# Softcapped attention with two feed-forward blocks: batches of three key chunks, the sums' transfers on GpSimd's queue, and a new order of VectorE's work at the end of attention

## The chip, the cores and the metric

The kernel runs on one core of a Trainium2 chip. The metric is the device time of one execution in microseconds (us), as the median of the runs. Times of single instructions come from one execution that the hardware profiler recorded; they count from the start of its span. The engines are called TensorE (PE in the profile; PEld is its loading of weights), VectorE (DVE), ScalarE (ACT), GpSimd (POOL) and SyncE (SP).

## What is computed

```
scores = (q @ k.T) / sqrt(64)                 # q, k, v: (2, 12, 448, 64), f32
scores = cap * tanh(scores / cap)             # cap = 30
attn   = exp(scores - max); attn /= attn.sum() + 1e-9
x      = attn @ v, laid out as 896 tokens x 768
x      = square(relu(x @ w_in)) @ w_out       # 768 -> 2048 -> 768
x      = silu(x @ w2_in) @ w2_out             # 768 -> 2048 -> 768
```

## The kernel before

Since the cap bounds the scores, the kernel leaves the maximum out: it takes exp(cap * tanh) and adds a constant, `gcap`, to the sums of the exponentials. The 24 heads are 12 pairs, i = 0 to 11. The 448 keys of a pair fall into three chunks of 128 and one of 64; the 64 last keys of two pairs share one chunk. So two pairs, one u = 0 to 5, have seven chunks, n = 0 to 6: n = 0 to 2 are the first pair's, n = 3 is the short shared one, n = 4 to 6 are the second pair's. There are 42 chunks, numbered here 0 to 41 (chunk 7u + n).

The order of the work is written out by hand. `batches` cuts the 42 chunks into 21 batches of two, and the loop over h goes one step per batch:

- `scores` (L274): TensorE multiplies keys and queries of a batch's chunks into tiles `s`, of which there are two (two PSUM banks each). ScalarE then runs tanh on each chunk (L282, from `s` to a tile `e` in SBUF), and after all chunks of the batch exp on each (L285, in place). A chunk's product must wait until the tanh of the chunk two before it has read its `s`.
- `evacuate` (L356): VectorE copies the finished product `px` of a pair that ended two steps ago to SBUF (`sb`).
- `add` (L315, L318, L321): VectorE adds the `e` of a pair together into `tot`, so that fewer products are needed for the sums.
- `values` (L296): TensorE multiplies the `e` of the batch before with the values into `px`.
- `add_up` (L333; L339 for the last two pairs) and `evacuate_sums` (L365): TensorE sums `tot` and the third `e` over the keys by a product with ones, VectorE copies the row of sums to `sm`, and SP's queue gathers it into a small tile `st` (L371), 56 numbers in each of 32 partitions for a group of two pairs.
- `invert` (L379 to L382) and `fetch` (L389), two steps after a group's second pair: VectorE forms the reciprocal of the small tile, SP's queue writes it to `scratch` in DRAM, and, once that has landed, reads it back spread over the partitions as `rb`.
- `normalise` (L396 to L399), some steps later: VectorE multiplies `sb` with `rb` and splits the result into two parts, `x0`, the input of the first feed-forward block.
- Up to two steps of the conversion of the first weights `u_wa` (L127 to L146), from 64-bit to 32-bit floats.

`GROUPS` holds the pairs 0 to 9. For pairs 10 and 11 (`LATE`) the sums are made in all partitions (L339) and inverted there, 128 x 448, on VectorE (L361, L362). On SP's queue the loads of the next queries, keys and values (L223, L224, L231) and of weights (L162) stand in one row with the sums' transfers; each instruction in it starts when the one ahead has been issued. After the loop follow the last products, sums and normalisations, and the first feed-forward block (L579) takes the first three units for the first batch entry alone (pairs 0 to 5).

Of the kernel before, what the change touches and what calls it, by code (L numbers as in the profile page):

```python
# [13 lines left out]
ALU = mybir.AluOpType  # L14
# [13 lines left out]
def softcap_attention_relu2_silu(  # L28
# [30 lines left out]
    NH = B * H  # L59
    GROUPS = ((0, 2), (2, 4), (4, 6), (6, 8), (8, 10))  # L60
    LATE = 10
    SCALE = 1.0 / float(D) ** 0.5
# [170 lines left out]
    def attention_bounded(att, ws, x0):  # L233
# [23 lines left out]
        parts = [(u, n) for u in range(NP2 // 2) for n in range(NU)]  # L257
        batches = [parts[n : n + 2] for n in range(0, len(parts), 2)]

# [7 lines left out]
        def scores(batch):  # L267

            for u, n in batch:
                sp = bank2(f"s{u}_{n}")  # L270
                for i, rows, keys in pieces(u, n):
                    for j in range(2):
                        p = slice(64 * j, 64 * j + 64)
                        nc.tensor.matmul(  # L274
                            sp[rows, j, :S],
                            lhsT=pr.qk[i][p, 1, keys],
                            rhs=pr.qk[i][p, 0],
                            start=True,
                            stop=True,
                        )  # L280
                t = att.tile([128, 2, S], F32, tag="e", bufs=7, name=f"e{u}_{n}")
                nc.scalar.activation(t, sp[:, :, :S], AF.Tanh, scale=scale_s)  # L282
                ex[u, n] = t
            for u, n in batch:
                nc.scalar.activation(ex[u, n], ex[u, n], AF.Exp, scale=scale_c)  # L285
# [18 lines left out]
        def add(batch):  # L304
            for u, n in batch:
                i = pieces(u, n)[0][0]
                e = ex[u, n]
                if i == NP2 - 1:
                    if n == NU - 1:
                        t = att.tile([128, 2, S], F32, tag="tot", bufs=3, name=f"tot{i}")  # L310
                        nc.vector.tensor_tensor(t, ex[u, n - 1], e, op=ALU.add)
                        tot[i] = [ex[u, NF + 1], t]
                elif n in (1, NF + 2):
                    t = att.tile([128, 2, S], F32, tag="tot", bufs=3, name=f"tot{i}")
# [10 lines left out]
        def add_up(i):  # L325
# [11 lines left out]
            for n, t in enumerate(tot[i]):  # L337
                for j in range(2):
# [6 lines left out]
                    )  # L345

        group = {i: gi for gi, (a, z) in enumerate(GROUPS) for i in range(a, z)}

# [9 lines left out]
        def evacuate_sums(i):  # L358
# [11 lines left out]
            for n in range(2):  # L370
                nc.sync.dma_start(  # L371
                    st[gi][8 * r : 8 * r + 16, n],
# [3 lines left out]
        def invert(gi):  # L376
# [4 lines left out]
            nc.vector.reciprocal(t, t)  # L381
            nc.sync.dma_start(scratch[2 * a : 2 * z].rearrange("r (a f) -> (r a) f", a=8), t)  # L382

        def fetch(gi):
# [3 lines left out]
            for j in range(2):  # L388
                nc.sync.dma_start(t[64 * j : 64 * j + 64], rows[j : j + 1].to_broadcast([64, z - a, S]))  # L389
            for i in range(a, z):  # L390
# [15 lines left out]
        todo = []  # L406
        loads = {0: 0, 2: 1, 4: 2, 8: 3, 12: 4, 16: 5}
        conversions = {4: 0, 8: 1, 12: 2}
        nb = len(batches)
# [6 lines left out]

        for h in range(nb + 1):
            if h < nb:
                scores(batches[h])
                for u, n in batches[h]:  # L420
                    if u + 1 < NP2 // 2:
                        if n in (1, 2):
                            pr.load(2 * u + 1 + n)
                        if n == 2:
                            pr.load_v(u + 1, FIRST)
                        if n == NF + 1:
                            pr.load_v(u + 1, SECOND)
                    if (u, n) == (0, 0):
                        pr.load_v(0, SECOND)
            if h == 1:  # L430
# [6 lines left out]
            for i in ended:  # L437
                evacuate(i)
            if h == nb:
                for i in ended:  # L440
                    add_up(i)
                add(batches[h - 1])
                due(h)
                break
            if h > 0:
                add(batches[h - 1])
                values(batches[h - 1])
                if (NP2 // 2 - 1, NF + 1) in batches[h - 1]:

                    e, u = ex[NP2 // 2 - 1, NF + 1], NP2 // 2 - 1  # L450
                    nc.vector.tensor_tensor(e[64:], e[64:], ex[u, NF][64:], op=ALU.add)
            for i in ended:
                add_up(i)
                evacuate_sums(i)
                for gi, (a, z) in enumerate(GROUPS):
                    if i == z - 1:
                        todo.append((lambda gi=gi: invert(gi), h + 2))
                        todo.append((lambda gi=gi: fetch(gi), h + 2))
                        for n in range(a, z):
                            todo.append((lambda n=n: normalise(n), h + 4 + 2 * (n - a)))  # L460
            if h in loads:
                ws.load_to(loads[h])
            due(h)
            if h in conversions:
                ws.convert_to(conversions[h], False)
                ws.split_to(conversions[h], False, nc.vector)
            if h == 16:
                ws.convert_to(3, False)
            ws.step(2)
        i = NP2 - 1  # L470
        values(batches[-1])
        add_up(i)
        evacuate_sums(i - 1)
        normalise(i - 1)
        due(99)
        evacuate_sums(i)
        sb[i] = px.pop(i)[:, :S]
# [251 lines left out]
```

## Time and profile before

| | us |
|---|---|
| median of 3 runs | 570.29 (568.53 to 572.13) |
| the profiled execution, its time | 571.89 |
| its span, first to last instruction | 570.1 |
| TensorE busy | 557.8 (98%) |
| VectorE busy | 409.6 (72%) |
| ScalarE busy | 251.3 (44%) |
| GpSimd busy | 1.0 (0%) |

Attention takes the span's first 97.56 us, then the feed-forward blocks begin. A view by windows gives for each stretch the busy time of each engine and the clock granted to TensorE (1.00 is 2.4 GHz, 0.50 is 1.2 GHz). The timeline lists instructions in order of time, neighbours of one kind merged into one line with their count; in brackets is how long the engine sat idle before, and what ended that. The chain of waits follows the work back from the last instruction to what released it.

### The profile page before, as it was taken

What the parts mean: (1) busy time and instruction counts of PE and PEld (TensorE: products, weight loads), DVE (VectorE), ACT (ScalarE), POOL (GpSimd) and SP (SyncE); (2) the same over time, 40 slices, a digit from 0 to 9 for tenths busy, and PEclk for the clock granted to TensorE, in tenths of its full rate; (3) what the DMA queues carried; (4) which work ended last, traced back from release to release, by engine and by line L of the source; (5) the groups of instructions that cost most, each with busy time, mean ns of one, the idle gap of its engine ahead of it and who ended that gap; (6) DMA issues with size and microseconds to landing.
All of it is one profiled execution on the core that took longest, in us unless ns stands there. A gap on an engine that the chain in (4) does not pass through costs nothing.

```text
span 570.1 us, 7396 instructions
## 1 busy us (share of the span) xinstructions
PE 557.8 (98%) x2896; PEld 469.8 (82%) x2896; DVE 409.6 (72%) x617; ACT 251.3 (44%) x376; POOL 1.0 (0%) x6
## 2 busy tenths in 40 slices
PE   9999897999999999999999999999999999999996
PEld 3323233999999999999999999999999999999996
DVE  1679999879988877667665768888888885547501
ACT  6998891156444443332332444454445522222101
POOL 0000000000000000000000000000000000000000
PEclk9999998999999999999999999999999999999999
DMA  8535550313333223333334443333343464345002
GB/s 271 170 96 159 170 170 19 85 56 112 110 112 111 75 74 112 103 119 116 105 94 148 124 154 91 102 102 103 109 109 108 110 166 119 105 155 164 1 0 102
DMA packets 51429, 64.30 MB, mean 113 GB/s; under 512 B 2746, under 2 KB 46522, under 8 KB 51386
## 3 DMA queue, kind: packets, MB, share of 16 engines
q1 hardware_dynamic: 51064, 63.36, 37.0%
q8 instruction: 24, 0.39, 0.3%
q10 hardware_dynamic: 290, 0.39, 0.2%
q14 instruction: 19, 0.16, 0.1%
q0 software_dynamic: 32, 0.00, 0.0%
HBM read 60.88 MB, written 2.79 MB: 112 GB/s over the span
## 4 chain that ended last, share of the span: by engine, by line
PE 89%; DVE 5%; DMA 4%; issue 1%; SPq 0%; ACT 0%; ACTq 0%; DVEq 0%
PE o_2f L658 6%; PE o_0f L658 6%; PE ha_0f L579 5%; PE ha_1f L579 5%; PE y_0f L579 5%; PE y_1f L579 5%; PE hc_1f L579 5%; PE hc_0f L579 5%; PE y0f L579 3%; PE y2f L579 3%; PE y4f L579 3%; PE o_6f L658 3%; PE o_5f L658 3%; PE o_4f L658 3%; PE s L274 2%; PE px L296 2%
## 5 line engine op out<-in xcount | busy, mean ns | idle before, releaser
L282 ACT ACTIVATE e<-s 128x896 f32<-128x896 f32 x42 | 36.8, 918 | 12.4 <-PE s L274 8.4
L285 ACT ACTIVATE e<-e 128x896 f32<-128x896 f32 x42 | 37.7, 955 | 0.0
L608 DVE TENSOR_TENSOR ra_0f<-ra_0f 128x448 f32<-128x448 f32 x16 | 9.9, 622 | 7.9 <-ACT ra_0f L606 7.9
L676 DVE COPY ob_0f<-o_0f 128x384 f32<-128x384 f32 x2 | 1.1, 558 | 17.2 <-PE o_0f L658 17.2
L606 ACT ACTIVATE rc_0f<-hc_0f 128x448 f32<-128x448 f32 x8 | 4.4, 546 | 20.1 <-PE hc_0f L579 20.1
L315 DVE TENSOR_TENSOR tot<-e,e 128x896 f32<-128x896 f32 x11 | 11.9, 1084 | 0.5 <-ACT e L285 0.5
L674 ACT ACTIVATE ob_1f<-o_0f 128x384 f32<-128x384 f32 x2 | 1.0, 492 | 25.6 <-PE o_0f L658 25.6
L606 ACT ACTIVATE ra_0f<-ha_0f 128x448 f32<-128x448 f32 x8 | 4.3, 542 | 16.8 <-PE ha_0f L579 16.8
L396 DVE TENSOR_TENSOR rb<-sb,rb 128x448 f32<-128x448 f32 x10 | 6.2, 622 | 6.2 <-DMA rb<-scratch 5.0
L141 ACT ACTIVATE hl_wb_2f<-u_wb_2f 128x512 fp32r<-128x512 f32 x6 | 3.8, 632 | 15.0 <-DVE u_wb_2f L134 15.0
L608 DVE TENSOR_TENSOR ra_1f<-ra_1f 128x448 f32<-128x448 f32 x16 | 9.9, 619 | 0.6 <-ACT ra_1f L606 0.6
L141 ACT ACTIVATE hl_wb_3f<-u_wb_3f 128x512 fp32r<-128x512 f32 x6 | 3.8, 632 | 14.8 <-DVE u_wb_3f L134 14.8
L333 PE MATMUL sum<-tot,ones 128*32 128x448 f32 x40 | 9.5, 551 | 0.0
L333 PE MATMUL sum<-e,ones 128*32 128x448 f32 x40 | 9.5, 551 | 0.0
L141 ACT ACTIVATE hl_wb_0f<-u_wb_0f 128x512 fp32r<-128x512 f32 x6 | 3.8, 630 | 12.5 <-DVE u_wb_0f L134 12.5
L639 ACT ACTIVATE x1f<-y_0f 128x448 fp32r<-128x448 f32 x3 | 1.6, 546 | 14.8 <-PE y_0f L579 14.8
L640 DVE TENSOR_TENSOR x1f<-y_0f,x1f 128x448 fp32r<-128x448 f32 x3 | 1.9, 624 | 8.4 <-ACT x1f L639 8.4
L579 PE MATMUL ha0f<-x0f,hl_wa0f 128*128 128x448 f32 x36 | 7.7, 368 | 0.0
L579 PEld LDWEIGHTS ha0f<-x0f,hl_wa0f 128*128 128x128 f32 x36 | 6.7, 188 | 1.2 <-issue 0.7
L579 PE MATMUL ha2f<-x0f,hl_wa2f 128*128 128x448 f32 x36 | 7.6, 365 | 0.0
L579 PE MATMUL hc4f<-x1f,hl_wc4f 128*128 128x448 f32 x36 | 7.5, 365 | 0.0
L579 PE MATMUL ha6f<-x0f,hl_wa6f 128*128 128x448 f32 x36 | 7.5, 365 | 0.0
(987 smaller groups left out, 1738.6 us busy)
## 6 DMA issues: line engine op xcount, KB each, us to landing
raw_wb_0f<-in_moe_w_out SPq DMA_DIRECT2D x6, 512.0 KB
raw_wb_1f<-in_moe_w_out SPq DMA_DIRECT2D x6, 512.0 KB
raw_wb_2f<-in_moe_w_out SPq DMA_DIRECT2D x6, 512.0 KB, 3.6
raw_wb_3f<-in_moe_w_out SPq DMA_DIRECT2D x6, 512.0 KB
rb<-scratch SPq DMA_DIRECT2D x10, 224.0 KB
raw_wd_0f<-in_moe_w_out SPq DMA_DIRECT2D x2, 768.0 KB
raw_wd_1f<-in_moe_w_out SPq DMA_DIRECT2D x2, 768.0 KB
raw_wd_2f<-in_moe_w_out SPq DMA_DIRECT2D x2, 768.0 KB
```

The source lines that it names most:

```text
L141: first = lambda: nc.scalar.activation(hl[:, 0], u, AF.Copy)
L274: nc.tensor.matmul(sp[rows, j, :S], lhsT=pr.qk[i][p, 1, keys], rhs=pr.qk[i][p, 0], start=True, stop=True,)
L282: nc.scalar.activation(t, sp[:, :, :S], AF.Tanh, scale=scale_s)
L285: nc.scalar.activation(ex[u, n], ex[u, n], AF.Exp, scale=scale_c)
L296: nc.tensor.matmul(px[i][64 * j : 64 * j + 64, :S], lhsT=pr.vt[u][rows, n, j], rhs=ex[u, n][rows, j], start=first, stop=last,)
L315: nc.vector.tensor_tensor(t, ex[u, n - 1], e, op=ALU.add)
L333: nc.tensor.matmul(sums[i][p : p + 32, :S], lhsT=ones[:, :32], rhs=t[:, j], start=True, stop=True)
L396: nc.vector.tensor_tensor(r, sb.pop(i), r, op=ALU.mult)
L579: nc.tensor.matmul(a, lhsT=hl[:, e_w, kk], rhs=mv[:, e_x], start=(first and e_w == 0 and e_x == 0), stop=(last and e_w == 1),)
L606: nc.scalar.activation(r, accs[f][b], func)
L608: nc.vector.tensor_tensor(r, r, r, op=ALU.mult)
L658: nc.tensor.matmul(acc[t], lhsT=g2[kf][:, e_g, t * 128 : t * 128 + 128], rhs=hl[:, e_w, kk], start=(kf == 0 and e_g == 0 and e_w == 0), st ...
```

## The change

A batch has three chunks, so the loop has 14 steps. There are ten tiles `e` and not seven; `s` keeps two. The sums' transfers of the first four groups (pairs 0 to 7) go to GpSimd's queue. `invert` and `fetch` come one step after a group's second pair, `normalise` three and four steps after, with the last ones held to steps 13 and the end. Loads and conversions of weights stand at other steps, three conversion steps to a step. Pair 10 is a group of its own with the small reciprocal. Pair 11's `tot` is formed as the others' are. Behind the loop the order is written anew.

```diff
-    GROUPS = ((0, 2), (2, 4), (4, 6), (6, 8), (8, 10))
-    LATE = 10
+    GROUPS = ((0, 2), (2, 4), (4, 6), (6, 8), (8, 10), (10, 11))
+    LATE = 11
...
-        batches = [parts[n : n + 2] for n in range(0, len(parts), 2)]
+        batches = [parts[n : n + 3] for n in range(0, len(parts), 3)]
...
-                t = att.tile([128, 2, S], F32, tag="e", bufs=7, name=f"e{u}_{n}")
+                t = att.tile([128, 2, S], F32, tag="e", bufs=10, name=f"e{u}_{n}")
...
-                if i == NP2 - 1:
-                    if n == NU - 1:
-                        t = att.tile([128, 2, S], F32, tag="tot", bufs=3, name=f"tot{i}")
-                        nc.vector.tensor_tensor(t, ex[u, n - 1], e, op=ALU.add)
-                        tot[i] = [ex[u, NF + 1], t]
-                elif n in (1, NF + 2):
+                if n in (1, NF + 2):
...
+        def queue(gi):
+
+            return nc.gpsimd if gi < 4 else nc.sync
...
-                nc.sync.dma_start(
+                queue(gi).dma_start(
                     st[gi][8 * r : 8 * r + 16, n],
...
-            nc.sync.dma_start(scratch[2 * a : 2 * z].rearrange("r (a f) -> (r a) f", a=8), t)
+            queue(gi).dma_start(scratch[2 * a : 2 * z].rearrange("r (a f) -> (r a) f", a=8), t)
...
-                nc.sync.dma_start(t[64 * j : 64 * j + 64], rows[j : j + 1].to_broadcast([64, z - a, S]))
+                queue(gi).dma_start(t[64 * j : 64 * j + 64, : z - a], rows[j : j + 1].to_broadcast([64, z - a, S]))
...
-        loads = {0: 0, 2: 1, 4: 2, 8: 3, 12: 4, 16: 5}
-        conversions = {4: 0, 8: 1, 12: 2}
+        loads = {0: 0, 1: 1, 3: 2, 6: 3, 8: 4}
+        conversions = {3: 0, 5: 1, 8: 2}
...
-            if h == nb:
-                for i in ended:
-                    add_up(i)
-                add(batches[h - 1])
-                due(h)
-                break
...
-                        todo.append((lambda gi=gi: invert(gi), h + 2))
-                        todo.append((lambda gi=gi: fetch(gi), h + 2))
+                        todo.append((lambda gi=gi: invert(gi), h + 1 if gi < 4 else nb))
+                        todo.append((lambda gi=gi: fetch(gi), h + 1 if gi < 4 else nb))
                         for n in range(a, z):
-                            todo.append((lambda n=n: normalise(n), h + 4 + 2 * (n - a)))
+                            at = h + 3 + n - a
+                            if at > nb - 2:
+
+                                at = nb - 1 if n == a and gi < 4 else nb
+                            todo.append((lambda n=n: normalise(n), at))
...
-            ws.step(2)
+            ws.step(3)
         i = NP2 - 1
+        last = GROUPS[-2]
+        add_up(i - 1)
+        add(batches[-1])
         values(batches[-1])
         add_up(i)
+
+        todo = [f for f, _ in todo]
+        late = [todo.pop() for _ in range(last[1] - last[0])][::-1]
+        inverted = [todo.pop() for _ in range(2)][::-1]
+        for f in inverted:
+            f()
+        evacuate(i - 1)
         evacuate_sums(i - 1)
+        for f in todo:
+            f()
+        invert(len(GROUPS) - 1)
+        fetch(len(GROUPS) - 1)
+        evacuate_sums(i)
+        for f in late:
+            f()
         normalise(i - 1)
-        due(99)
-        evacuate_sums(i)
         sb[i] = px.pop(i)[:, :S]
         normalise(i)
```

Three places show how the instructions stand. First TensorE at the end of the loop before: products of scores (`s`), with values (`px`) and with ones (`sum`), the last of u = 5, chunks 38 to 41.

```order
L274 MATMUL s_3_728<-qk10f 64x448 x2
L274 MATMUL s_3_728<-qk11f 64x448 x2
L274 MATMUL s_4_735<-qk11f 128x448 x2
L296 MATMUL px_721<-e_1_710,vt5f 64x448 x2
L296 MATMUL px_721<-e_2_715,vt5f 64x448 x2
L333 MATMUL sum_750<-tot_681,ones 32x448 x2
L333 MATMUL sum_750<-e_6_670,ones 32x448 x2
L274 MATMUL s_5_762<-qk11f 128x448 x2
L274 MATMUL s_6_767<-qk11f 128x448 x2
```

The same engine and place now, the last step of the loop and the sums of pair 10 behind it:

```order
L274 MATMUL s_4_734<-qk11f 128x448 x2
L274 MATMUL s_5_739<-qk11f 128x448 x2
L274 MATMUL s_6_744<-qk11f 128x448 x2
L296 MATMUL px_711<-e_1_685,vt5f 64x448 x2
L296 MATMUL px_711<-e_2_690,vt5f 64x448 x2
L296 MATMUL px_711<-e_3_697,vt5f 64x448 x2
L296 MATMUL px_763<-e_3_697,vt5f 64x448 x2
L328 MATMUL sum_766<-tot_704,ones 32x448 x2
L328 MATMUL sum_766<-e_6_645,ones 32x448 x2
L328 MATMUL sum_778<-tot_754,ones 32x448 x2
L328 MATMUL sum_778<-e_2_690,ones 32x448 x2
```

Three chunks of scores follow each other where two did, and three of values.

Second, VectorE at the end before: pair 9's `sb` and pair 10's first addition, the sums of pair 9, the normalisation of pair 6 (`rb_702`), then the last additions of pairs 10 and 11.

```order
L356 COPY sb_742<-px_656 128x448 [waits PE_49]
L315 TENSOR_TENSOR tot_744<-e_0_675,e_1_710 128x896 [waits Activation_49]
L365 COPY sm_755<-sum_750 128x448 [waits PE_49]
L396 TENSOR_TENSOR rb_702<-sb_569,rb_702 128x448 [waits DMAHW7_49,DMAHW0_49]
L398 TENSOR_SCALAR x0f<-rb_702 128x448 [waits DVE_49]
L399 TENSOR_TENSOR x0f<-rb_702,x0f 128x448 [waits DVE_49]
L321 TENSOR_TENSOR tot_744<-tot_744,e_3_733 64x896 [waits Activation_49]
L451 TENSOR_TENSOR e_4_738<-e_4_738,e_3_733 64x896 [waits PE_49,Activation_49]
L356 COPY sb_783<-px_721 128x448
L311 TENSOR_TENSOR tot_790<-e_5_765,e_6_770 128x896 [waits Activation_49]
```

The same engine now: the inversion of pairs 6 and 7 ends step 12; step 13 holds `sb` of pair 9, pair 10's `tot`, the sums of pair 9 and the normalisation of pair 6 (`rb_731`, which that inversion's transfers bring); then comes `tot` of pair 11.

```order
L378 TENSOR_TENSOR st_627<-st_627 32x56 [waits DMASW6_49,DMASW7_49,DMASW1_49,DMASW0_49]
L379 TENSOR_SCALAR st_627<-st_627,gcap 32x56 [waits DVE_49]
L380 RECIPROCAL st_627<-st_627 32x56 [waits DVE_49]
L355 COPY sb_752<-px_662 128x448
L310 TENSOR_TENSOR tot_754<-e_0_650,e_1_685 128x896 [waits Activation_49]
L316 TENSOR_TENSOR tot_754<-tot_754,e_3_697 64x896 [waits DVE_49,Activation_49]
L364 COPY sm_771<-sum_766 128x448 [waits PE_49]
L395 TENSOR_TENSOR rb_731<-sb_609,rb_731 128x448 [waits DMASW4_49,DMASW3_49]
L397 TENSOR_SCALAR x0f<-rb_731 128x448 [waits DVE_49]
L398 TENSOR_TENSOR x0f<-rb_731,x0f 128x448 [waits DVE_49]
L310 TENSOR_TENSOR tot_783<-e_4_737,e_5_742 128x896 [waits Activation_49]
L313 TENSOR_TENSOR tot_783<-tot_783,e_3_697 64x896 [waits DVE_49,Activation_49]
```

The additions of pair 10 stand ahead of pair 6's normalisation where one stood behind it, and pair 11's stand behind it.

Third, SP's queue before, where the queries and keys of pair 8 (`qk8f`) stand behind the transfers of the sums of pairs 2 to 4:

```order
L371 DMA st_450<-sm_448 16x1x56 [waits DMAHW0_49,DVE_49]
L371 DMA st_450<-sm_448 16x1x56 [waits DMAHW1_49]
L382 DMA scratch<-st_342 32x56 [waits DMAHW4_49,DMAHW2_49,DVE_49]
L389 DMA rb_457<-scratch 64x2x448 [waits DMAHW3_49,DMAHW2_49]
L389 DMA rb_457<-scratch 64x2x448
L223 DMA qk8f<-in_q 128x448 [waits DMAHW5_49,PE_49]
L224 DMA qk8f<-in_k 128x448 [waits DMAHW6_49]
```

SP's queue now at the same load:

```order
L224 DMA qk7f<-in_k 128x448 [waits DMAHW1_49]
L231 DMA vt3f<-in_v 128x512 [waits DMAHW2_49]
L231 DMA vt3f<-in_v 128x384 [waits DMAHW3_49]
L162 DMA raw_wa3f<-in_moe_w_in 128x6x256 [waits DMAHW4_49,DVE_49,Activation_49]
L223 DMA qk8f<-in_q 128x448 [waits DMAHW5_49,PE_49]
L224 DMA qk8f<-in_k 128x448 [waits DMAHW6_49]
```

Only loads stand ahead of it; the sums' transfers of pairs 0 to 7 are on GpSimd's queue.

## Rows read from the trace of the kernel before

**Rows 1.** View by windows: stretch, length, busy per engine, granted clock (PEclk), DMA.
```profile
20.40:57.70 37.30, 37.30 (x218) 11.05 (x216) 28.40 (x43) 33.95 (x41) 0.00 (x0) 1.00 0.51 155
87.30:91.20 3.90, 0.01 (x1) 0.00 (x0) 2.89 (x6) 2.40 (x3) 0.00 (x0) 1.00 0.02 5
...
93.00:94.00 1.00, 1.00 (x6) 0.34 (x4) 1.00 (x2) 0.00 (x0) 0.00 (x0) 0.50 0.00 0
```

**Rows 2.** Waits of TensorE over the span: us in total, times, longest.
```profile
PE sum L339 <- DVE tot L321: 3.9, 1, 3.9
```

**Rows 3.** Chain of waits, early steps: start, us, what.
```profile
12.74 1.81 PE px L296 x12
...
16.25 1.65 PE px L296 x8
17.91 0.89 PE sum L333 x8
...
26.56 1.71 PE s L274 x8
```

**Rows 4.** Timeline, PE's last sums and the feed-forward block's first products.
```profile
95.95 0.92 PE L339 MATMUL sum<-e,ones 128*64 128x448 f32 x4
...
96.71 0.92 PE L339 MATMUL sum<-tot,ones 128*64 128x448 f32 x4
...
97.56 3.92 PE L579 MATMUL ha0f<-x0f,hl_wa0f 128*128 128x448 f32 x18
```

**Rows 5.** Timeline, one batch of scores on PE and its tanh and exp.
```profile
68.18 1.77 PE L274 MATMUL s<-qk9f 64*128 64x448 f32 x8
...
69.25 1.73 ACT L282 ACTIVATE e<-s 128x896 f32<-128x896 f32 x2 [0.88 <-PE s L274]
...
70.86 1.79 ACT L285 ACTIVATE e<-e 128x896 f32<-128x896 f32 x2
```

**Rows 6.** Timeline, the loop's first two batches.
```profile
6.47 1.73 ACT L282 ACTIVATE e<-s 128x896 f32<-128x896 f32 x2 [3.67 <-PE s L274]
...
7.44 1.55 PE L274 MATMUL s<-qk0f 64*128 64x448 f32 x6 [0.27 <-ACT e L282]
```

**Rows 7.** Timeline, PE: the first scores of pair 8.
```profile
59.53 1.77 PE L274 MATMUL s<-qk8f 64*128 64x448 f32 x8 [1.74 <-DMA qk8f<-in_k]
```

**Rows 8.** Timeline, DVE: small reciprocal, weight conversion, pairs 6 and 10, large reciprocal.
```profile
80.57 0.20 DVE L379 TENSOR_TENSOR st<-st 32x56 f32<-32x56 f32 x1
...
81.50 0.48 DVE L128 TENSOR_SCALAR u_wa3f<-u_wa3f 128x768 int32<-128x768 int32 x1
82.02 0.96 DVE L131 SCALAR_TENSOR_TENSOR u_wa3f<-raw_wa3f,u_wa3f 128x768 int32<-128x768 int32 x1
...
88.44 0.62 DVE L396 TENSOR_TENSOR rb<-sb,rb 128x448 f32<-128x448 f32 x1 [0.91 <-DMA rb<-scratch]
...
90.07 1.08 DVE L321 TENSOR_TENSOR tot<-tot,e 64x896 f32<-64x896 f32 x1
91.18 1.09 DVE L451 TENSOR_TENSOR e<-e,e 64x896 f32<-64x896 f32 x1
...
97.12 2.95 DVE L362 RECIPROCAL sm<-sm 128x448 f32<-128x448 f32 x1
```

**Rows 9.** Chain of waits: the reciprocal's way through DRAM and back.
```profile
38.36 4.95 DMA rb<-scratch
...
70.77 4.18 DMA rb<-scratch
...
81.75 1.38 DMA scratch<-st
...
83.15 0.64 SPq L389
```

**Rows 10.** Timeline: the one transfer on GpSimd's queue.
```profile
1.24 0.66 POOL L91 DMA_DIRECT2D capt<-in_cap  x1 [0.79 <-POOLq L707]
...
6.13 0.15 DVE L432 TENSOR_SCALAR gcap<-capt 128x1 f32<-128x1 f32 x1 [3.68 <-DMA capt<-in_cap]
```

More of the change, by code (lines that the diff above doesn't have):

```diff
@@ L415, in due @@
                     todo.remove((f, at))
[L417 to L429, printed above, removed]
+        for h in range(nb):
+            scores(batches[h])
+            for u, n in batches[h]:
+                if u + 1 < NP2 // 2:
+                    if n in (1, 2):
+                        pr.load(2 * u + 1 + n)
+                    if n == 2:
+                        pr.load_v(u + 1, FIRST)
+                    if n == NF + 1:
+                        pr.load_v(u + 1, SECOND)
+                if (u, n) == (0, 0):
+                    pr.load_v(0, SECOND)
             if h == 1:
@@ L447, in attention_bounded @@
                 values(batches[h - 1])
-                if (NP2 // 2 - 1, NF + 1) in batches[h - 1]:
-                    e, u = ex[NP2 // 2 - 1, NF + 1], NP2 // 2 - 1
-                    nc.vector.tensor_tensor(e[64:], e[64:], ex[u, NF][64:], op=ALU.add)
             for i in ended:
@@ L466, in attention_bounded @@
                 ws.split_to(conversions[h], False, nc.vector)
-            if h == 16:
+            if h == 10:
                 ws.convert_to(3, False)
-            ws.step(2)
+            ws.step(3)
         i = NP2 - 1
+        last = GROUPS[-2]
+        add_up(i - 1)
+        add(batches[-1])
         values(batches[-1])
         add_up(i)
-        evacuate_sums(i - 1)
+        todo = [f for f, _ in todo]
[4 more added lines that the diff above has]
+        evacuate(i - 1)
+        evacuate_sums(i - 1)
+        for f in todo:
[5 more added lines that the diff above has]
+            f()
         normalise(i - 1)
-        due(99)
-        evacuate_sums(i)
         sb[i] = px.pop(i)[:, :S]
```

## The prediction

> **What bounds the kernel now.** I read the view by windows first. From 20.40 to 57.70 us TensorE is busy for 37.30 of 37.30 us while ScalarE has 33.95 and VectorE 28.40 [rows 1]: attention is bound by TensorE, closely followed by ScalarE. The feed-forward blocks, 472 us of the span, are bound by TensorE too, and the change leaves their products as they are. So what counts is when their first product starts, at 97.56 before [rows 4], and whether VectorE then keeps up. The list of TensorE's waits shows one large hole, 3.9 us for `tot` on VectorE [rows 2], and the windows show it from 87.30 to 91.20, with the granted clock at 0.50 afterwards [rows 1]. The timeline tells why: VectorE stood still for 0.91 us until `rb` came, normalised pair 6 and only then added pair 10 [rows 8]. A second hole of 1.74 us is the late arrival of `qk8f` [rows 7].
>
> What do these holes cost? Behind 91.20 there remain the sums of pair 10, two chunks of values and the sums of pair 11. Such sums take 1.61 us (95.95 to 97.56) [rows 4], two chunks of values 1.65 [rows 3], together 4.87; they took 6.36. The fallen clock thus cost 1.5 us.
>
> **TensorE's price list.** Two chunks of scores take 1.71 us until the next group starts, two of values 1.65, the sums of a pair 0.89; a short chunk adds 0.16 (1.81 for 1.65) [rows 3]. One more chunk of the same kind costs 0.76 (95.95 to 96.71, four products) [rows 4]. So a change of kind costs 1.71 - 1.52 = 0.19 for scores and 0.13 for values. 14 groups of each and not 21 would save 7 x 0.32 = 2.2 us. That is what larger batches could give.
>
> **What larger batches cost.** There are still two tiles `s`. With two chunks to a batch, every product found its tile already read by the batch before. The third chunk of a batch must instead wait for the tanh of the first chunk of its own batch. That tanh starts 1.07 us after the batch's first product (68.18 to 69.25) [rows 5], and a product that waited for a tanh starts 0.97 after the tanh's start (6.47 to 7.44) [rows 6]. So the third chunk starts 2.04 us into the step and not after 1.52, and the values start at 2.04 + 0.76 + 0.19 = 2.99. With 2.41 for three chunks of values a step takes 5.40 us, 6.29 with a pair's sums. Three chunks cost 1.5 x (1.71 + 1.65) = 5.04 before. ScalarE does not bind: its last exp ends about 6.4 into the step (tanh at 1.07 and 1.99, the third at 3.11, then three exps, of which two take 1.79 [rows 5]), ahead of the next first tanh at 5.40 + 1.07.
>
> The start is dearer. ScalarE runs the third tanh at 7.44 + 1.07 = 8.5 to 9.4 and three exps to 12.0; only then comes the tanh of chunk 3, which chunk 5 waits for. So chunk 5 starts at 13.0, the first values at 13.9, step 2 at 16.3. In step 2 the exps of chunks 3 to 5 end at 17.6, the third chunk starts at 18.6, its values at 19.5 and step 3 at 22.1 (19.5 + 2.41 + 0.16). Before, six chunks of values and eight of scores were done at 17.91 [rows 3]; with a ninth, 18.7. The start costs 3.4 us.
>
> Steps 3 to 12: ten at 5.40, nine sums at 0.89 and six short chunks at 0.16 make 63.0. Step 13 starts at 85.1, and I call this time t13. The wait of 1.74 for `qk8f` is not in it: its load no longer stands behind the transfers of the sums, and only loads are ahead of it on SP's queue, and the tile that it fills is free three steps before it is wanted.
>
> **The end, on VectorE.** The reciprocal of pairs 6 and 7 is formed in step 12, behind the copy of pair 8's sums. In that step VectorE is late. It copies pair 7's sums to 0.8 us after the step's start (0.18 until they are ready, 0.62), normalises pair 4 (1.63, from 88.44 to 90.07), converts weights (0.48 + 2 x 0.96), copies `sb` (taken as 0.62, the product of that size) and adds pair 9 (two at 1.11) [rows 8]. That ends 7.65 into a step of 6.45, at t13 + 1.2. The copy of pair 8's sums, the normalisation of pair 5 and the small reciprocal (0.93, from 80.57 to 81.50) follow, to t13 + 4.4.
>
> The reciprocal then goes to DRAM and back. On SP's queue this took 1.38 + 0.64 and then 4.18 to 4.95 [rows 9], with 0.2 ahead of it 6.4 to 7.2 us; I take 6.8. Now it goes by GpSimd's queue. The trace has one transfer there, `capt`, issued at 1.24 and used at 6.13 [rows 10]: 4.9 us, 3.5 more than the 1.38 of a small transfer on SP's queue. So each of the two hops in a row costs between 0 and 3.5 more. I take 1.0, nearer to SP's rows, since `capt` ran among the loads of the start, and at 87 to 91 us the DMA engines were nearly idle (share 0.02) [rows 1]. That makes 8.8 and `rb_731` at t13 + 13.2. VectorE is done with `sb` of pair 9, pair 10's `tot` and pair 9's sums at t13 + 7.9 and stands still until then. Behind it wait pair 6's normalisation and pair 11's `tot`: 13.2 + 1.63 + 2.22 = t13 + 17.0, 102.1 us.
>
> TensorE ends the loop at 91.5, waits a little for pair 10's `tot` (t13 + 7.2), and has done pair 10's sums and the last values at 95.6. Then it stands still for 6.5 us until pair 11's `tot` comes. Its sums take 1.6, the clock costs 1.5 again, so the feed-forward block starts in effect at 105.2, 7.6 us later than before.
>
> **What the end saves.** Pair 10's sums cost 0.89 and not 1.61, which is in the numbers above, and one large reciprocal of 2.95 us [rows 8] leaves VectorE's chain. That gives nothing as long as VectorE keeps ahead of TensorE. Behind pair 11's `tot` it has two small reciprocals, two copies, five normalisations and one large reciprocal with its addition: 1.9 + 1.2 + 8.2 + 3.5 = 14.8 us. TensorE wants pair 11's `x0` only 1.6 + 1.5 + 14 us after that `tot`: three units for the first batch entry, 3.65 each (18 products; 3.92 with the last one's end [rows 4]), and five sixths of the fourth. No new wait follows.
>
> **The sum.** The loop ends at 91.5 where it ended at 87.3: + 4.2. Of this the start gives 3.4 and eleven steps at 0.36 give 4.0, `qk8f` takes 1.74 away, and the rest is that one chunk of values fewer (0.8) is done by then and that sums and short chunks fall differently. From the loop's end to the block's start it takes 13.7 us where it took 10.3: + 3.4. Together + 7.6 us. The profiled execution took 571.89, which would become 579.5; it lies 1.6 above the median of 570.29. For the median I forecast 577.9.
>
> The Trainium skill (DMA: Bandwidth & Descriptors, Latency and other measured facts) gives the first byte 0.6 us after a start from SyncE and about 1 us from GpSimd. By it each hop would cost 0.4 more and the time would be 576.7; that is an estimate from the page, and no row here shows it.
>
> **The rivals.**
> - *The third chunk does not wait* (not slower). If chunk 3 of a batch found its tile free, steps would take 4.88 and not 5.40, and the start would cost nothing: 3.4 + 10 x 0.52 = 8.6 us less on TensorE, and as VectorE's work at the end hangs on TensorE's sums, 569.3, which is no change. It decides from a wait below about 0.2 us per step. For it: the two groups saved are real [rows 3]. Against: 1.07 and 0.97 are measured, and the tile count is two.
> - *`rb_731` comes in time* (within 1%). If the round trip takes under 3.5 us, VectorE does not stand still, `tot` of pair 11 is there at t13 + 11.7 = 96.8, TensorE waits 1.2 us, the clock stays, and the block starts at 98.4: 571.2. Against: the quickest trip on SP's queue took 6.4 [rows 9]. Both of these together would give 562.5, faster by 1.4%.
> - *GpSimd's transfers are slow.* At 3.5 us more per hop `rb_731` comes 5 us later still: 582.9. For it: the one row of that queue [rows 10]. The Trainium skill speaks for it too (DMA: Bandwidth & Descriptors, SWDGE vs HWDGE vs iDMA): GpSimd writes its descriptors to SBUF, where VectorE in its two-port mode locks it out, and SyncE's never go that way. No row here shows such a lock.
> - *The queue gives nothing.* If `qk8f` still came late, + 1.7: 579.6. Against: in the order now, nothing but loads is ahead of it.
>
> **How the numbers follow.** The main case, 577.9, has a chance of 0.48, with a range of its own from 574 (a quick round trip of 6.4 and a start 1.5 us cheaper) to 582; about a third of it lies below 576, 1% above the median. The slow queue has 0.14, the late `qk8f` 0.04. No wait of the third chunk 0.12, the transfer in time 0.14, both 0.08. A measurement of this kernel can tell about 1% from no change. Slower by more than that: 0.32 + 0.14 + 0.04 = 0.50; within 1%: 0.16 + 0.12 + 0.14 = 0.42; faster 0.08. The range from 568.5 to 583 leaves out the case of both and a part of the slow queue.
>
> **What would show it.** Right: ScalarE's tanh of a batch's third chunk starts about 1 us behind its second one; steps of 5.4 and 6.3 us, step 13 at about 85; VectorE idle for some 5 us before pair 6's normalisation with `rb` from `scratch` as what ended it; TensorE idle for 4 us or more before the sums of pair 11 (L334), with the granted clock at 0.50 behind; L586 starting after 101. Wrong: a batch's three groups of scores follow each other in 2.5 us; no wait of VectorE for `rb` at the end; the first product of the feed-forward block before 98 us; or stalls of VectorE for `x0` or `hl_wa3f` later, of which I count none.

## The result, and the profile of the changed kernel

The changed kernel took 578.71 us (median of 4 runs, 577.20 to 579.83) beside 571.21 for the kernel before in the same runs: ratio 1.0117, 95% interval 1.0069 to 1.0165. It is slower; 577.9 was forecast. The profiled execution took 579.83 with a span of 578.0, 7.9 more than the span before. In some executions TensorE's products took 2% longer through the feed-forward blocks (7.44 us for 36 of them in the profiled ones of e4_two_norm_late and e5_two_slack, 7.30 here, each at a granted clock of 1.00) while attention's did not, and as ratios and medians are over executions of both kinds, small differences between them decide nothing below.

TensorE's waits in the changed kernel (us in total, times, longest), where [rows 2] showed one hole of 3.9 and [rows 7] one for `qk8f`:

```profile
PE s L274 <- ACT e L282: 4.9, 11, 2.3
PE sum L334 <- DVE tot L313: 4.4, 1, 4.4
PE sum L328 <- DVE tot L316: 0.7, 1, 0.7
```

The wait for `qk8f` is gone. New are eleven waits of the scores for a tanh, each of the third chunk of a batch (there are fourteen batches); the longest is in the second step. The timeline of TensorE at the start shows it (start, duration, instruction, idle time before it and what ended it), where [rows 6] had only 0.27:

```profile
7.11 1.55 PE L274 MATMUL s<-qk0f 64*128 64x448 f32 x6 [0.27 <-ACT e L282]
...
12.47 1.86 PE L274 MATMUL s<-qk1f 64*128 64x448 f32 x4 [2.27 <-ACT e L282]
14.26 3.24 PE L296 MATMUL px<-e,vt0f 128*64 128x448 f32 x12
...
19.47 1.02 PE L274 MATMUL s<-qk2f 64*128 64x448 f32 x4 [0.27 <-ACT e L282]
...
22.99 1.55 PE L274 MATMUL s<-qk2f 64*128 64x448 f32 x6
```

Behind the long wait the same kind of work is slow: the values at 14.26 take 3.24 us, later ones of that size 2.48. The view by windows (columns as in [rows 1]) says why, here and at the end; the level 0.50 is 1.2 GHz:

```profile
13.00:14.00 1.00, 1.00 (x4) 0.00 (x0) 0.00 (x0) 0.22 (x1) 0.00 (x0) 0.50 1.09 366
...
103.00:104.00 1.00, 1.00 (x4) 0.00 (x0) 0.93 (x3) 0.00 (x0) 0.00 (x0) 0.50 0.01 1
```

Then the end, on the timeline of all engines (answering to [rows 4, 8, 9]):

```profile
86.03 1.77 PE L274 MATMUL s<-qk11f 64*128 64x448 f32 x8
...
90.08 0.49 DVE L380 RECIPROCAL st<-st 32x56 f32<-32x56 f32 x1
...
90.87 0.51 POOL L381 DMA_DIRECT2D scratch<-st  x1 [9.03 <-DVE st L380]
...
92.76 1.20 POOL L388 DMA_DIRECT2D rb<-scratch  x2 [1.39 <-DMA scratch<-st]
...
93.29 0.57 PE L328 MATMUL sum<-tot,ones 128*32 128x448 f32 x2 [0.74 <-DVE tot L316]
...
97.12 0.62 DVE L395 TENSOR_TENSOR rb<-sb,rb 128x448 f32<-128x448 f32 x1 [3.35 <-DMA rb<-scratch]
...
99.87 1.09 DVE L313 TENSOR_TENSOR tot<-tot,e 64x896 f32<-64x896 f32 x1
...
101.10 1.73 PE L334 MATMUL sum<-tot,ones 128*64 128x448 f32 x4 [4.45 <-DVE tot L313]
...
103.55 1.35 SPq L388 DMA_DIRECT2D rb<-scratch  x2
...
104.26 4.06 PE L586 MATMUL ha0f<-x0f,hl_wa0f 128*128 128x448 f32 x18
105.14 1.16 SPq L370 DMA_DIRECT2D st<-sm  x2
107.98 0.20 DVE L378 TENSOR_TENSOR st<-st 16x56 f32<-16x56 f32 x1 [3.36 <-DMA st<-sm]
...
118.96 0.30 PEld L586 LDWEIGHTS ha0f<-x0f,hl_wa0f 128*128 128x128 f32 x2 [0.47 <-DVE x0f L398]
```

VectorE stands 3.35 us until pair 6's `rb` is there; pair 11's `tot` stands behind it; TensorE idles 4.45 us and then runs at half clock. All that was in the forecast. Not in it: VectorE stands another 3.36 us at 107.98, because pair 10's transfer `st<-sm` on SP's queue was issued only behind the fetch at 103.55. It cost TensorE 0.47 us at `x0`.

### The profile page after: what moved, and what is told of

The parts are those of the page before. It is cut to its first block, busy times and chain, and to the rows that moved or that the text cites. A ratio compares the mean times of both kernels' runs of the same rounds, so it can differ in the third digit from the quotient of the medians.

```text
span 578.0 us, 7419 instructions
## 1 busy us (share of the span) xinstructions
PE 560.6 (97%) x2896; PEld 469.9 (81%) x2896; DVE 407.6 (71%) x619; ACT 252.6 (44%) x376; POOL 18.0 (3%) x34
## 4 chain that ended last, share of the span: by engine, by line
PE 88%; ACT 4%; DVE 3%; issue 2%; DMA 2%; SPq 0%; POOL 0%; DVEq 0%; ACTq 0%
PE o_0f L665 6%; PE o_2f L665 6%; PE ha_1f L586 5%; PE hc_1f L586 5%; PE hc_0f L586 5%; PE y_0f L586 5%; PE y_1f L586 5%; PE ha_0f L586 4%; PE px L296 4%; PE s L274 4%; PE y4f L586 3%; PE y2f L586 3%; PE y0f L586 3%; PE o_6f L665 3%; PE o_5f L665 3%; PE o_4f L665 3%
## 5 line engine op out<-in xcount | busy, mean ns | idle before, releaser
L364 DVE COPY sm<-sum 128x448 f32<-128x448 f32 x11 | 6.8, 620 | 9.8 <-PE sum L328 9.7
L370 POOL DMA_DIRECT2D st<-sm x16 | 9.5, 600 | 50.0 <-DVE sm L364 44.5
L141 ACT ACTIVATE hl_wb_3f<-u_wb_3f 128x512 fp32r<-128x512 f32 x6 | 3.8, 632 | 14.8 <-DVE u_wb_3f L134 14.8
L328 PEld LDWEIGHTS sum<-tot,ones 128*32 128x32 f32 x44 | 1.6, 108 | 8.6 <-issue 2.8
L646 ACT ACTIVATE x1f<-y_0f 128x448 fp32r<-128x448 f32 x3 | 1.6, 545 | 14.8 <-PE y_0f L586 14.8
```

Of the source, the lines that this page charges most:

```text
L141: first = lambda: nc.scalar.activation(hl[:, 0], u, AF.Copy)
L328: nc.tensor.matmul(sums[i][p : p + 32, :S], lhsT=ones[:, :32], rhs=t[:, j], start=True, stop=True)
L370: queue(gi).dma_start(st[gi][8 * r : 8 * r + 16, n], t[64 * n : 64 * n + 64 : 32].rearrange("o (a f) -> o a f", a=8),)
```

## The experiments

Theory A, after the result: the third chunk's wait costs the loop 4 us and more, pair 6's place on VectorE costs the end another 5 to 6, and the queue as such costs nothing. Line numbers are the changed kernel's. Ratios are to the kernel before, on the same chip.

**e1_norm_late**

```
-                                at = nb - 1 if n == a and gi < 4 else nb
+                                at = nb
```

> The changed kernel, with pair 6 normalised after the loop and not in its last step, so that on VectorE pair 11's `tot` no longer stands behind the wait for `rb_731`. Theory A (that order makes the hole before the last sums): pair 11's `tot` ends near 96 us and not 100.96, TensorE goes from its last values (end 96.7) to the sums of pair 11 (L334) with less than 0.5 us idle, the granted clock stays at 1.00 there, and the block's first product starts near 98.3 and not 104.26. VectorE then wants 1 to 1.5 us more of TensorE's time at the second batch entry's `x0` (0.47 in the changed kernel), so the time falls by about 5 us, to +2.5 us over the kernel before (ratio 1.004). Rival (the transfer itself is what is late, whatever stands behind it): TensorE idles 3 us or more elsewhere, at pair 10's sums or at `x0`, and the ratio stays above 1.009.

577.04 us, ratio 1.0099 [1.0063, 1.0134]. The hole is gone and the first product stands at 98.50, as theory A said, 5.8 us earlier. But the span fell by 3.1 only, and the ratio, forecast at 1.004, is where the rival put it (above 1.009) and not clear of the changed kernel's. Timeline:

```profile
95.21 1.09 DVE L313 TENSOR_TENSOR tot<-tot,e 64x896 f32<-64x896 f32 x1
96.90 0.92 PE L334 MATMUL sum<-tot,ones 128*64 128x448 f32 x4
...
98.50 3.91 PE L586 MATMUL ha0f<-x0f,hl_wa0f 128*128 128x448 f32 x18
...
104.62 0.20 DVE L378 TENSOR_TENSOR st<-st 16x56 f32<-16x56 f32 x1 [1.77 <-DMA st<-sm]
...
115.60 0.82 PE L586 MATMUL ha0f<-x0f,hl_wa0f 128*128 128x448 f32 x2 [0.19 <-DVE x0f L398]
116.22 5.26 PE L586 MATMUL ha_1f<-x0f,hl_wa1f 128*128 128x448 f32 x18
```

TensorE got ahead of VectorE, waited piece by piece for `x0` (1.4 us in six waits, not the 3 of the rival), and its clock fell behind that (granted 0.50 from 116 to 119 us): 5.26 for a unit of 3.81. The order made the hole, but only about half of it was to be had: VectorE's idle time for small transfers (1.29 and 1.77 us) was the next bound.

**e2_sync**

```
-            return nc.gpsimd if gi < 4 else nc.sync
+            return nc.sync
```

> The changed kernel, with all transfers of the sums back on SP's queue. Theory A (the queue is worth only what it frees in front of the loads): the round trip from reciprocal to `rb` is as long as on GpSimd's queue (6.5 us) within 0.7, the wait for `qk8f` may come back (up to 1.7 us), and the time is 0 to 1.7 us above the changed kernel, ratio 1.012 to 1.015. Rival (GpSimd's transfers are slow and cost the end 2 us or more): `rb_731` lands 2 us or more sooner, the hole of VectorE (3.35) shrinks by as much, and the ratio falls to 1.008 or less.

580.00 us, ratio 1.0144 [1.0109, 1.0179], against 1.0117 [1.0069, 1.0165] of the changed kernel: no difference that these intervals show. VectorE's wait for pair 6's `rb` is 3.6 us (3.35), and no wait for `qk8f` is there. So in this order of work the queue costs and gives nothing that can be seen here (the spans are 578.2 and 578.0). Its rival falls.

```profile
DVE rb L395 <- DMA rb<-scratch: 3.6, 1, 3.6
```

**e3_two**

```
-        batches = [parts[n : n + 3] for n in range(0, len(parts), 3)]
+        batches = [parts[n : n + 2] for n in range(0, len(parts), 2)]
...
+                        todo.append((lambda gi=gi: invert(gi), h + 2 if gi < 4 else nb))
+                        todo.append((lambda gi=gi: fetch(gi), h + 2 if gi < 4 else nb))
...
+                            at = h + 4 + 2 * (n - a)
```

> The changed kernel with batches of two chunks again (and the load and conversion steps of the kernel before); queue and end stay changed. Pair 6 is normalised in the last but one step, ahead of pair 10's last `tot`, as in the kernel before. Theory A (the third chunk's wait for the tanh of its own batch, at the start and in each step, costs the loop 4.2 plus the 1.7 that the queue gives back): no wait for `qk8f`, the third step's scores start near 18.7 worth of work as before, TensorE ends its loop at 85.6 (kernel before 87.3, changed 91.5), a hole of 3 to 4 us before pair 10's sums remains, and the time is 1 to 2.5 us below the kernel before, ratio 0.9955 to 0.998. Rival (the larger batches do not matter, the end alone costs): ratio above 1.006.

576.70 us, ratio 1.0120 [1.0059, 1.0181]: theory A missed by 8 to 9 us, and the rival's number came. Its reason is not what the trace shows. There are no waits for a tanh and none for `qk8f`, but two holes for a `tot`, one in the middle of the loop:

```profile
61.34 0.63 DVE L395 TENSOR_TENSOR rb<-sb,rb 128x448 f32<-128x448 f32 x1 [3.55 <-DMA rb<-scratch]
...
63.44 1.08 DVE L316 TENSOR_TENSOR tot<-tot,e 64x896 f32<-64x896 f32 x1
...
64.57 0.57 PE L328 MATMUL sum<-tot,ones 128*32 128x448 f32 x2 [3.46 <-DVE tot L316]
...
94.79 0.96 PE L328 MATMUL sum<-tot,ones 128*32 128x448 f32 x2 [4.21 <-DVE tot L316]
```

It is the same fault as at the end, a normalisation that waits for `rb` ahead of a `tot`, now in the middle.

**e4_two_norm_late**

```
-                            if at > nb - 2:
+                            if at > nb - 2 or gi == 3:
```

(with the edits of e3_two and e1_norm_late)

> Batches of two, queue and end as changed, and pairs 6 and 7 normalised after the loop. Theory A (two separate costs that add: batches, and order on VectorE at the end): no hole before pair 10's or pair 11's sums longer than 1 us, clock at 1.00 there, the block's first product near 91.5 (97.56 before), an `x0` wait of 0.5 to 2 us at the second batch entry, time 5 to 7 us below the kernel before, ratio 0.988 to 0.991. Rival (VectorE is the bound of the end, whatever the order): TensorE waits for `x0` what it no longer waits for `tot`, and the ratio stays at 0.995 or above.

Ratio 1.0052 [1.0009, 1.0095], not 0.988 to 0.991 but where the rival put it. The last hole went, as expected (first product at 95.90 where 91.5 was forecast, and 0.58 us before pair 10's sums); the one near 64 us stayed with 3.43, and `x0` took 0.7, much less than the rival's reason asks for. Theory A lacked two costs. Theory B takes them in: the third chunk's wait, a normalisation too early for its `rb`, and a small transfer behind SP's queue, each by itself.

**e8_before_queue**: the kernel before, with the three kinds of transfers of pairs 0 to 7 on GpSimd's queue, nothing else.

```
-                nc.sync.dma_start(
+                (nc.gpsimd if gi < 4 else nc.sync).dma_start(
                     st[gi][8 * r : 8 * r + 16, n],
...
```

> The kernel before with nothing changed but the queue: the transfers of pairs 0 to 7's sums on GpSimd's. Theory B (as in e3_two: the loads no longer wait, so `qk8f` is in time, but the sums' transfers run beside those loads and pair 4's `rb` lands 2 us or more later behind its issue than on SP's queue, on which VectorE waits ahead of pair 7's `tot`): the wait of 1.74 for `qk8f` is gone, a hole of some 3.5 us for `tot` near 64 us is there, with the granted clock at 0.50 to 0.6 behind it, and the time is 2 to 4 us above the kernel before, ratio 1.004 to 1.007. Rival (the queue alone gives what it frees): no such hole, 1 to 2 us below the kernel before, ratio 0.997.

578.16 us, ratio 1.0091 [1.0040, 1.0141], above even what theory B gave. The queue alone, with batches of two, costs nearly as much as the whole change. The chain of waits, and on the timeline SP's weight loads:

```profile
52.54 1.64 DMA scratch<-st
55.08 6.70 DMA rb<-scratch
72.69 1.64 DMA scratch<-st
75.24 5.14 DMA rb<-scratch
```

```profile
53.07 0.38 SPq L162 DMA_DIRECT2D raw_wa4f<-in_moe_w_in  x1
...
73.28 0.38 SPq L162 DMA_DIRECT2D raw_wa5f<-in_moe_w_in  x1
```

On SP's queue `rb` took 4.18 to 4.95 [rows 9], and the weight loads were issued behind it. Here they were issued 1.4 and 1.3 us ahead of its issue at 54.46 and 74.62 (before the first also the loads of `qk10f`), and it took 6.70 and 5.14; the two fetches without such a load ahead took 4.07 and 4.26. From 54 to 61 us the DMA engines' share was 0.98. The same fetch took 6.33 to 6.60 in e3_two, e4_two_norm_late, e5_two_slack and e9_two_hop, each time 1.3 to 1.4 us behind a weight load. The wait for `qk8f` is gone, but VectorE's waits for `rb` grew from 5.0 us to 11.7, and behind them came holes at TensorE for `tot` (2.7 near 65 us, 4.6 at the end). A third hole came by way of ScalarE, whose tanh waited until VectorE's `tot` had read a tile `e`:

```profile
65.02 0.57 PE L333 MATMUL sum<-tot,ones 128*32 128x448 f32 x2 [2.69 <-DVE tot L321]
...
84.28 0.92 ACT L282 ACTIVATE e<-s 128x896 f32<-128x896 f32 x1 [3.62 <-DVE tot L315]
...
85.25 1.02 PE L274 MATMUL s<-qk11f 64*128 64x448 f32 x4 [2.23 <-ACT e L282]
```

The fall of the clock that theory B put behind the hole near 65 us did not come: the granted clock stayed at 1.00.

**e5_two_slack and e6_three_early**: in both, pair 10's sums are sent first at the end, on GpSimd's queue; e5_two_slack has batches of two and pairs 0 to 5 normalised a step later, e6_three_early batches of three.

```
-            return nc.gpsimd if gi < 4 else nc.sync
+            return nc.sync if gi == 4 else nc.gpsimd
...
+        evacuate_sums(i - 1)
+        evacuate(i - 1)
         for f in inverted:
             f()
-        evacuate(i - 1)
-        evacuate_sums(i - 1)
...
+                            at = min(h + 5 + 2 * (n - a), nb - 3) if gi < 3 else nb   # e5_two_slack
+                            at = nb   # for at > nb - 2, e6_three_early
```

> Batches of two; pairs 0 to 5 are normalised a step later than in e3_two and e4_two_norm_late, pairs 6 and 7 behind the loop; at the end pair 10's sums are copied and sent first, by GpSimd's queue. Theory B (three costs that add: the third chunk's wait, VectorE standing still for `rb` ahead of a `tot`, and VectorE standing still for pair 10's small transfer behind SP's queue): no TensorE hole over 1 us at pair 7's or later sums (3.43 at 64.29 us in e4_two_norm_late), clock 1.00 there, first product of the block near 91, `x0` waits under 1 us in all, time 4 to 7 us below the kernel before, ratio 0.988 to 0.993. Rival (VectorE as a whole is short of time, and a hole closed in one place opens in another): a new hole of 2 us or more, ratio above 0.996.

> e1_norm_late (batches of three, pair 6 normalised behind the loop) with pair 10's sums copied and sent first at the end, by GpSimd's queue: the same end as e5_two_slack, with batches of three. Theory B: VectorE's idle for `st` (1.29 and 1.77 us in e1_norm_late) falls below 0.5 in all, the `x0` waits of TensorE and the clock's fall behind them (together 4 us there) go, time 3 to 4.5 us below e1_norm_late, ratio 1.001 to 1.004; and it stays 5 to 8 us above e5_two_slack, which is what batches of three cost in the loop. Rival 1 (VectorE's work, not its waits, is the bound at `x0`): ratio 1.008 or more. Rival 2 (the batches cost nothing once the end is in order): within 1 us of e5_two_slack.

Ratios 0.9985 [0.9924, 1.0045] and 1.0141 [1.0095, 1.0187], both outside theory B's forecasts and where their rivals put them (above 0.996, and 1.008 or more). The loop of e5_two_slack is what theory B wants: no hole over 1.2 us in it, and an early first product (97.56 before):

```profile
90.89 3.92 PE L583 MATMUL ha0f<-x0f,hl_wa0f 128*128 128x448 f32 x18
```

Both lose at one new place, a wait for `x0` of 2.43 and 2.77 us. Timeline of e6_three_early:

```profile
99.85 0.53 SPq L162 DMA_DIRECT2D raw_wa5f<-in_moe_w_in  x1
...
100.43 0.54 SPq L162 DMA_DIRECT2D raw_wa6f<-in_moe_w_in  x1
...
101.23 0.51 POOL L381 DMA_DIRECT2D scratch<-st  x1 [4.79 <-DVE st L380]
...
108.57 1.07 POOL L388 DMA_DIRECT2D rb<-scratch  x2 [6.83 <-DMA scratch<-st]
111.81 0.62 DVE L395 TENSOR_TENSOR rb<-sb,rb 128x448 f32<-128x448 f32 x1 [4.20 <-DMA rb<-scratch]
...
112.92 0.47 PE L586 MATMUL ha0f<-x0f,hl_wa0f 128*128 128x448 f32 x1 [2.77 <-DVE x0f L397]
```

With nothing of pair 10 left on SP's queue, the weight loads were issued earlier, and behind its small reciprocal, issued 1.4 and 0.8 us after them, GpSimd's queue stood for 6.83 us until it had landed, and not for 1.39. e5_two_slack shows the same with 6.50, e7_start_two with 7.72.

**e7_start_two**

```
+        batches = [parts[n : n + 2] for n in range(0, 6, 2)] + [parts[n : n + 3] for n in range(6, len(parts), 3)]
```

(on e6_three_early, the steps of loads and conversions shifted by one)

> e6_three_early with the first six chunks in batches of two and the other 36 in batches of three. Theory B (of the price of the larger batches some 3.4 us or more lie in the first three steps, where ScalarE has three exps between a batch's third tanh and the next batch's first): the wait of 2.27 us at chunk 5 and the granted clock of 0.50 behind it go, the step that begins with chunk 9 starts near 19 us and not 23, time 3 to 4.5 us below e6_three_early, ratio 0.993 to 0.998. Rival (the price is spread over all steps, or ScalarE only makes up later for what it did not do early): under 1.5 us below e6_three_early.

Ratio 1.0042 [0.9985, 1.0100]. That is about 1% below e6_three_early by the ratios and 0.4% by the medians (577.04 for 579.27), but the traces don't bear out theory B: the first product came 1.05 us earlier (95.45 for 96.50), and the step from chunk 9 on began at 20.48 against 21.40, not near 19. The rival fits the traces: ScalarE takes part of the gain back later (the third chunk at 28.67 us waits 1.01 for its tanh, the same one of e6_three_early 0.27), and the start's share of the price is about 1 us when the clock holds. Against e5_two_slack (90.89) the twelve remaining batches of three cost 4.56 us, 0.38 each (0.45 if one counts that e5_two_slack waited 0.9 us longer for `tot`). The times can't decide it: TensorE's wait for `x0`, of the kind just shown, is 2.8 us in one and 3.9 in the other.

**e9_two_hop, e10_three_hop, e11_two_sync**: of pair 10's three transfers only the first stays on GpSimd's queue. e9_two_hop has batches of two, e10_three_hop batches of three; e11_two_sync is e9_two_hop with pairs 0 to 9 on SP's queue.

```
-            return nc.sync if gi == 4 else nc.gpsimd
+            return nc.gpsimd if gi < 4 else nc.sync   # e11_two_sync: return nc.sync
...
-                queue(gi).dma_start(
+                (nc.gpsimd if gi != 4 else nc.sync).dma_start(   # e11_two_sync: gi == 5
                     st[gi][8 * r : 8 * r + 16, n],
```

> e5_two_slack with one thing changed: of pair 10's three transfers at the end only the first, of its sums, stays on GpSimd's queue; its reciprocal to `scratch` and back go by SP's queue again, in front of the loads of `raw_wa5` and `raw_wa6`. Theory C (in e5_two_slack those two loads, 1.5 MB, were issued 0.8 and 1.4 us before the small transfer, which then took 6.50 us; in front of them it takes some 1.4): `scratch` lands within 2 us, VectorE's wait of 3.95 for `rb` and TensorE's of 2.43 for `x0` fall below 0.5 each, the first product stays near 91, time 2 to 4 us below e5_two_slack, ratio to the kernel before 0.990 to 0.995. Rival (a small transfer of that size is slow at that time on any queue): the waits stay above 2 us and the ratio is that of e5_two_slack.

> e6_three_early with the same change as e9_two_hop: batches of three, with the end of e9_two_hop. Theory C (batches of three cost the loop 4.4 to 5.6 us, 0.37 a step and 1 to 2 at the start, whatever the end): TensorE's wait of 2.77 for `x0` falls below 0.5, the first product stays near 96.5, time 4 to 6 us above e9_two_hop, ratio to the kernel before 1.000 to 1.004. Rival (the batches' cost is hidden once the end is free of waits, since VectorE's work behind the last `tot` is the longer chain): within 2 us of e9_two_hop.

> e9_two_hop with the transfers of pairs 0 to 9's sums on SP's queue, as in the kernel before; pair 10's sums alone go by GpSimd's. Theory C (the queue gives back the wait for `qk8f` and nothing else, once the normalisations come a step later): a wait of 1 to 1.8 us for `qk8f` or a later load, `rb` landing at 4 to 5 us, time 1 to 2 us above e9_two_hop. Rival 1 (GpSimd's transfers are the slower ones and cost VectorE more than the loads gain): 1 us or more below e9_two_hop. Rival 2 (the later normalisations free SP's queue too): no wait for loads, within 0.7 us of e9_two_hop.

e9_two_hop: 566.19 us, ratio 0.9892 [0.9850, 0.9934], faster than the kernel before and so than the changed one. e10_three_hop: 573.36, 1.0014 [0.9982, 1.0046]. e11_two_sync: 565.44, 0.9899 [0.9844, 0.9953]. Timeline of e9_two_hop:

```profile
86.30 0.57 PE L328 MATMUL sum<-tot,ones 128*32 128x448 f32 x2 [1.15 <-DVE tot L316]
...
90.35 3.98 PE L583 MATMUL ha0f<-x0f,hl_wa0f 128*128 128x448 f32 x18
...
94.73 0.31 SPq L381 DMA_DIRECT2D scratch<-st  x1
...
97.59 1.11 SPq L388 DMA_DIRECT2D rb<-scratch  x2
...
98.75 0.59 SPq L162 DMA_DIRECT2D raw_wa5f<-in_moe_w_in  x1
```

and of e10_three_hop:

```profile
11.76 1.02 PE L274 MATMUL s<-qk1f 64*128 64x448 f32 x4 [1.89 <-ACT e L282]
...
20.96 1.55 PE L274 MATMUL s<-qk2f 64*128 64x448 f32 x6
...
91.29 0.57 PE L328 MATMUL sum<-tot,ones 128*32 128x448 f32 x2 [0.77 <-DVE tot L316]
...
96.09 3.91 PE L586 MATMUL ha0f<-x0f,hl_wa0f 128*128 128x448 f32 x18
```

The end is now the same in both: the small transfer is issued ahead of the weight loads and lands 2.5 and 1.9 us behind its issue (theory C had 2), and TensorE's wait for `x0` is 0 and 0.47. So it was not VectorE's work that bound e5_two_slack and e6_three_early, as their rivals had it. What is left between them is the size of the batches, with the steps of loads, conversions and normalisations that go with it: pair 10's sums start 5.0 us apart (86.30 and 91.29), the first product 5.7, the medians 7.2, of which 4 to 6 were forecast. e11_two_sync answers for the queue: it is as fast (0.75 us less by the medians, 0.07% more by the ratios), without a wait for `qk8f`, and VectorE has no wait for `rb`; theory C's wait of 1 to 1.8 us did not come, and its second rival held. The queue decides nothing once the normalisations come late enough.

## Why the prediction was right

The forecast of 7.6 us over the kernel before (7.5 measured) names the right two causes, the third chunk's wait in the loop and pair 6's wait for `rb` at the end. That the total fits so well is luck in part, since its parts were off in both directions. In the profiled executions TensorE's loop ends 5.25 us later (92.55 for 87.30, where its wait for pair 10's `tot` begins) and not 4.2. From there to the block's first product it takes 1.45 us more (11.71 for 10.26) and not 3.4. Behind the first product another 1.2 us are lost (7.9 in the span, 6.7 at the first product), where the forecast had nothing. The steps:

- **Step length: right.** Step 3 began at 22.99 and step 13 at 86.03: 63.04 us, where 63.0 was worked out. e7_start_two against e5_two_slack gives 0.38 to 0.45 a step for the third chunk; 0.36 was forecast.
- **The start: size off, by a term that was missing.** Chunk 5 was forecast at 13.0 and step 3 at 22.1, 9.1 us later. Chunk 5 came at 12.47, step 3 only 10.5 us behind it, at 22.99. In e10_three_hop and e6_three_early, where the granted clock stayed at 1.00, it was 9.2 us (11.76 to 20.96, 12.20 to 21.40), as forecast. So the fall of the clock behind the wait cost 1.3 us. The forecast counted such a fall at the end and not here.
- **`qk8f`: the wait went, the reason was wrong.** It was put to the queue. On SP's queue it is gone too, with batches of three (e2_sync) and with batches of two and later normalisations (e11_two_sync). Before, its load was issued 3.9 us ahead of its product's turn (53.87 for 57.79) and was there 5.7 us later; in these two it was issued 10.9 and 4.8 us ahead. The rival "the queue gives nothing" was right about the queue and wrong about the time.
- **VectorE's lateness: right.** The small reciprocal ended at t13 + 4.5 (90.57 less 86.03); 4.4 was forecast.
- **The round trip: too long.** From there to `rb` it took 6.55 us (to 97.12), not 8.8, and in e2_sync on SP's queue 6.8. At this place the small transfer took 1.89 us from its issue to the next one's on GpSimd's queue (90.87 to 92.76) and 1.92 on SP's in e2_sync. Where no load was near, it landed 1.62 to 1.64 us behind its issue on GpSimd's queue (e8_before_queue) and 1.36 to 1.38 on SP's (kernel before). The way back took no longer either (4.36 us from its issue to VectorE's product, 4.81 in e2_sync). So 0.3 in one hop is the most that these runs show, and the 1.0 added to each has nothing to stand on. The Trainium skill (DMA: Bandwidth & Descriptors, Latency and other measured facts) has the first byte 0.4 us later from GpSimd; the traces agree in kind and show less.
- **The hole and the clock: right in kind.** TensorE idled 4.45 us before the last sums and 0.74 before pair 10's, where 6.5 and a little were forecast, for `rb` took 2 us less; the sums then took 3.16 us (101.10 to 104.26), twice [rows 4], which is the 1.5 for the clock.
- **"No new wait follows": wrong.** Pair 10's transfer stood behind the fetch on SP's queue, VectorE 3.36 us behind it. It hid behind the hole and cost 0.47 us; in e1_norm_late, where the hole is gone, it is the next bound. The sum of VectorE's work (14.8 us) was right, but it was a sum of work without its waits.
- **The rival of slow transfers on GpSimd's queue** was wrong for this place (DMA share 0.02 from 90.5 to 92.5 us, when the reciprocal was sent) and right beside loads: 6.70 us in e8_before_queue, 6.83 in e6_three_early. The lock of which the Trainium skill speaks (DMA: Bandwidth & Descriptors, SWDGE vs HWDGE vs iDMA) isn't needed for it: the slow transfers stood behind weight loads, and the others were not slow although VectorE worked beside them as well. Whether VectorE was in its two-port mode then, no trace here shows.

So the change as made costs 7.5 us, and e10_three_hop, which keeps the larger batches and mends the end, 0.8 (ratio 1.0014, from 1.0 us less to 2.6 more). What the larger batches cost is e10_three_hop against e9_two_hop, 5.7 us at the first product. That e9_two_hop lies below the kernel before has to do with VectorE's order, in which no normalisation stands in front of a `tot` before its `rb` is there; pair 10's cheaper sums (0.89 us for 1.61) and the wait for `qk8f` that is gone have a share in it too, and no run takes these apart.

What stays open: why the clock fell in the second step of the changed kernel and of e1_norm_late (TensorE idle for 2.27 and 2.30 us) and not in e6_three_early and e10_three_hop (2.07 and 1.89), nor behind the 2.69 us of e8_before_queue, and how often it does. Three tiles `s` for batches of three were not tried.

## What to carry to other kernels

Before making a batch larger, count its buffers: here, with two tiles, the third part waited in each step for the reader of the first, and that cost 0.38 us a step or more, with the changes between kinds of work that it saved already taken off. On an engine that works in order, put nothing that waits for a trip through DRAM ahead of work that the bound engine wants next: one step later left no such wait here, one step too early cost TensorE holes of 3.4 to 4.6 us, with the granted clock at 0.50 behind them. And when a queue is relieved, ask what it will issue earlier, since that runs beside what was moved.

## What was not expected of the hardware

A small transfer (32 or 16 rows of 56 numbers to DRAM) held GpSimd's queue for 1.38 to 1.72 us until it had landed when no load was issued just ahead or beside it, for 2.6 to 3.1 beside loads of queries and keys, and for 6.50, 6.83 and 7.72 us when two weight loads of 768 KB had been issued on SP's queue 1.4 and 0.8 us ahead of it (e5_two_slack, e6_three_early, e7_start_two). The order on one queue protected it; a queue of its own didn't.
